# Folding the inverse of modes 0 to 31 into x ahead of the channel product, and adding modes 32 to 63 on row halves in the last stage

## The chip, the cores and the metric

The kernel runs on one core of one Trainium2 chip. The metric is the device time of one execution in microseconds (us). A profile is one execution recorded by the hardware profiler; its span is about 2 us shorter than the device time of the same execution.

## The reference, cut to what matters

A linear attention gives x, a Fourier stage mixes the channels of the first 64 frequencies (modes), and a channel product with a rectifier follows.

```python
num = einsum('bhsd,bhde->bhse', phi(q), einsum('bhsd,bhse->bhde', phi(k), v))
den = einsum('bhsd,bhd->bhs', phi(q), sum(phi(k), axis=2)) + 1e-6
x = (num / den)                       # as [8 batches, 576 rows, 512 channels]
X = rfft(x, axis=1)                   # 64 modes are kept
Y[:, m] = X[:, m] @ (w_r[m] + 1j * w_i[m])      # 64 modes, 512 x 512 each
y = irfft(Y, n=576, axis=1)
u = x + y
out = u + maximum(u @ w_ch, 0)        # float32
```

The weights w_r and w_i are 64 x 2 x 1 MB in float32, by far the largest input. They are converted to bf16 as they are loaded, so 512 KB lands in on-chip memory for each.

## The kernel before

The first 100 us compute the attention and the forward transform. From then on the weights stream in through a ring of eight buffers, and each mode's product is made when its two weights have landed. In the shadow of that stream, 36 tiles of 128 rows and 512 channels are worked on. One tile computes its rows of x again and then forms its channel product E = x @ w_ch, without y:

```python
def channel_product(t):
    num = ...                                        # attention rows (TensorE)
    nc.vector.tensor_tensor(out=x, in0=num, in1=1/den, op=mult)
    nc.scalar.copy(out=x16, in_=x)                   # to f16
    for c in range(4):                               # four transposes
        nc.tensor.transpose(xT_ps[:, c, :], x16[:, c*128 : c*128+128], id16)
    nc.vector.tensor_copy(out=xT, in_=xT_ps)
    for c in range(4):                               # "eps": four products
        nc.tensor.matmul(e_ps, xT[:, c, :], wch16[:, c, :], ...)
    nc.scalar.copy(out=E[t], in_=e_ps)
```

The transform is linear, so y @ w_ch is the inverse transform of Z = Y @ w_ch. A "row building" (`form_rows`, one for each batch) makes Z by four products and y's rows by four transposes, and keeps both in YZ[b]. The last eight modes come too late for this; their rows are made at the very end in a tile called `last` and copied into the rows of YZ[b] by eight small transfers. The last stage then goes over 18 pairs of tiles:

```python
acc  = E                    # by a product with the identity
acc += inv^T @ Z[b]         # all 64 modes are 128 rows (real and imaginary part)
acc  = relu(acc)            # ScalarE
acc += inv^T @ Y[b]
x    = acc + x              # VectorE
store x                     # 512 KB for a pair
```

Where tiles and row buildings stand among the modes is written in this loop, but a scheduler decides the order in which each engine finally executes them, except for instructions that are marked with `pin`, which keep the order of the program:

```python
for kk in range(10, 64):
    mode(kk)                                   # pinned from mode 60 on
    want = min(36, (kk - 10 + 1) * 36 // 42)   # 36 tiles over modes 10 to 51
    while done < want:
        channel_product(tiles[done]); done += 1
    if kk >= 55:
        ...                                    # two row buildings for a mode
```

While the last four modes wait for their weights, 39 needless products (`keep_warm`, called fillers here; their result is never read) keep TensorE busy.

## Time and profile before

| before | | where it is read |
|---|---|---|
| time | 432.05 us, median of 3 (431.16 to 432.51) | the runs |
| span | 429.8 us | the page |
| share of the chain of waits that is DMA | 67% | the page, part 4 |
| a mode's two weight loads | 4.92 us | starts of neighbouring modes' products |
| last stage, from its first product with `last` to the end | 32.2 us (397.62 to 429.8) | the chain of waits |

These are lines of the page of before. In the first four, each place is one of 40 equal slices of the span: the busy share of TensorE and its granted clock in tenths, that of the DMA engines, and what these moved. The fifth line is the chain of waits by engine. The last is the stores of the pairs: how many, how large, and the median time in us from issue to landing.

```profile
PE   0358776887018776856886666778675758999993
PEclk9999666565558765566556678555658655999998
DMA  8999999999999999999999999999999999995697
GB/s 148 207 208 209 209 210 210 211 214 215 222 211 214 215 213 214 214 214 214 213 213 214 214 213 214 213 214 214 213 213 214 214 214 214 214 213 97 239 369 296
...
DMA 67%; PE 17%; issue 7%; DVE 4%; ACT 2%; POOL 1%; DVEq 0%; POOLq 0%; ACTq 0%
...
out_dram<-x_main SPq DMA_DIRECT2D x14, 512.0 KB, 3.1
```

The DMA engines are busy in every slice up to the 36th, which ends at 387 us, so up to there the kernel lasts as long as its weights. TensorE is mostly busy for 50 to 90% of a slice in that time, often at little over half its clock, and this costs nothing.

The chain of waits of before shows how the weights hand over to the last stage (start, duration in us, what):

```profile
340.80 19.27 DMA wi<-in_moe_w_i_dram
...
360.11 0.66 PE P L355 x3
360.77 1.82 PE eps L507 x4
362.59 1.71 PE z L530 x4
...
378.95 0.65 PE P L355 x5
```

The chain meets its last weight load at 360 us. After that TensorE always has work: the last tile (`eps`), eight row buildings (`z`), the last modes (`P`) and the fillers. It is hardly behind the weights; the last mode's product is done at 395.7 us.

In the last stage three limits lie close together. The timeline of before (start, duration, engine, line, operation, operands, count) shows it:

```profile
412.44 0.59 PE L593 MATMUL acc<-E,id 128*128 128x512 f16 x2
412.87 1.03 PE L549 MATMUL acc<-YZ,inv_sb 128*128 128x512 f16 x4
413.73 0.59 PE L593 MATMUL acc<-E,id 128*128 128x512 f16 x2
...
411.35 8.99 DVE L638 TENSOR_TENSOR x_main<-acc,x_main 128x1024 f32<-128x1024 f32 x7
```

A pair takes TensorE 413.73 - 412.44 = 1.29 us, and VectorE 8.99 / 7 = 1.28 us. The stores need 512 KB for a pair, which is 1.28 us at 408 GB/s, about the most that this trace has in a window of 2 us.

### The profile page before, as it was taken

What the parts mean: (1) busy time and instruction counts of PE and PEld (TensorE: products, weight loads), DVE (VectorE), ACT (ScalarE), POOL (GpSimd) and SP (SyncE); (2) the same over time, 40 slices, a digit from 0 to 9 for tenths busy, and PEclk for the clock granted to TensorE, in tenths of its full rate; (3) what the DMA queues carried; (4) which work ended last, traced back from release to release, by engine and by line L of the source; (5) the groups of instructions that cost most, each with busy time, mean ns of one, the idle gap of its engine ahead of it and who ended that gap; (6) DMA issues with size and microseconds to landing.
All of it is one profiled execution on the core that took longest, in us unless ns stands there. A gap on an engine that the chain in (4) does not pass through costs nothing.

```text
span 429.8 us, 6238 instructions
## 1 busy us (share of the span) xinstructions
PE 296.9 (69%) x2551; PEld 154.8 (36%) x2551; DVE 181.9 (42%) x373; ACT 146.6 (34%) x227; POOL 91.5 (21%) x165
## 2 busy tenths in 40 slices
PE   0358776887018776856886666778675758999993
PEld 0346555664003332322232222322222324954441
DVE  1699998955004233233232322332323322211694
ACT  3687666631002222222222322122212222311782
POOL 4232223222102312121112221221211121110200
PEclk9999666565558765566556678555658655999998
DMA  8999999999999999999999999999999999995697
GB/s 148 207 208 209 209 210 210 211 214 215 222 211 214 215 213 214 214 214 214 213 213 214 214 213 214 213 214 214 213 213 214 214 214 214 214 213 97 239 369 296
DMA packets 35803, 92.38 MB, mean 215 GB/s; under 512 B 3136, under 2 KB 16448, under 8 KB 35776
## 3 DMA queue, kind: packets, MB, share of 16 engines
q0 software_dynamic: 32000, 82.00, 98.2%
q1 hardware_dynamic: 3776, 10.00, 6.1%
q8 instruction: 20, 0.33, 0.3%
q14 instruction: 7, 0.06, 0.0%
HBM read 164.07 MB, written 9.44 MB: 404 GB/s over the span
## 4 chain that ended last, share of the span: by engine, by line
DMA 67%; PE 17%; issue 7%; DVE 4%; ACT 2%; POOL 1%; DVEq 0%; POOLq 0%; ACTq 0%
DMA wi<-in_moe_w_i_dram 33%; DMA wr<-in_moe_w_r_dram 22%; DMA k<-in_k_dram 11%; PE acc L549 4%; PE P L355 3%; PE z L530 2%; PE zl L340 2%; PE acc L593 2%; PE eps L507 2%; PE yp L534 1%; DVE x L272 1%; ACT ke L187 1%; DVE k L194 0%; ACT qT L223 0%; POOL q L169 0%
## 5 line engine op out<-in xcount | busy, mean ns | idle before, releaser
L507 PE MATMUL eps<-wch,xTw 128*128 128x512 f16 x144 | 62.3, 582 | 3.4 <-DVE xTw L504 3.1
L515 ACT CAST E<-eps 128x512 f16<-128x512 f32 (+1 forms) x40 | 21.3, 543 | 122.7 <-PE eps L507 122.7
L115 POOL DMA_DIRECT2D wr<-in_moe_w_r_dram x64 | 34.0, 531 | 135.5 <-PE P L355 109.4
L355 PE MATMUL P<-wi,xt_c 128*32 128x512 bf16 x252 | 42.1, 565 | 27.3 <-DMA wi<-in_moe_w_i_dram 27.3
L355 PE MATMUL P<-wr,xt_c 128*32 128x512 bf16 x252 | 42.6, 582 | 22.9 <-DMA wr<-in_moe_w_r_dram 20.9
L115 POOL DMA_DIRECT2D wi<-in_moe_w_i_dram x65 | 34.5, 531 | 108.5 <-PE P L355 74.1
L355 PEld LDWEIGHTS <-xt_c 128*32 128x32 bf16 x504 | 24.3, 163 | 67.8 <-issue 38.7
L369 DVE CAST ys<-P 128x512 f16<-128x512 f32 x32 | 22.0, 688 | 59.7 <-PE P L355 59.7
L151 PEld LDWEIGHTS <-qT 64*128 64x128 f16 (+1 forms) x640 | 21.5, 126 | 56.8 <-issue 41.8
L371 ACT CAST ys<-P 128x512 f16<-128x512 f32 x31 | 18.1, 585 | 63.2 <-PE P L355 63.0
L373 PE MATMUL yt<-pick_sb,ys 128*128 128x16 f16 x252 | 16.8, 177 | 31.6 <-DMA pick_sb<-row_pick 20.4
L504 DVE COPY xTw<-xTp 128x512 f16<-128x512 f16 x36 | 15.2, 423 | 51.8 <-PE xTp L502 51.8
L373 PEld LDWEIGHTS <-ys 128*128 128x128 f16 x252 | 12.3, 105 | 51.1 <-issue 23.4
L151 PE MATMUL num<-kv,qT 64*128 64x65 f16 (+1 forms) x320 | 14.0, 230 | 22.6 <-ACT kv L247 20.1
L507 PEld LDWEIGHTS <-xTw 128*128 128x128 f16 x144 | 14.7, 124 | 33.7 <-issue 24.2
L492 DVE TENSOR_TENSOR x_main<-nw,rd 128x256 f32<-128x256 f32 x32 | 12.1, 419 | 33.8 <-PE nw L151 33.7
L187 ACT ACTIVATE qe<-q 128x1152 f16<-128x1152 f16 x16 | 17.7, 1155 | 22.9 <-DMA q<-in_q_dram 22.9
L216 PE MATMUL qTp<-id,qe 128*128 128x128 f16 x144 | 16.6, 310 | 12.1 <-DVE qe L200 11.7
L499 ACT CAST x16w<-x_main 128x512 f16<-128x512 f32 x32 | 19.8, 619 | 14.2 <-DVE x_main L492 14.2
L272 DVE TENSOR_TENSOR x<-num,rd 128x512 f16<-128x512 f32 x32 | 22.1, 691 | 1.1
L491 DVE RECIPROCAL rdw<-nw 128x4 f32<-128x4 f32 (+1 forms) x40 | 5.5, 170 | 38.3 <-PE nw L151 38.2
L502 PE MATMUL xTp<-id,x16w 128*128 128x128 f16 x144 | 19.4, 278 | 2.8 <-ACT x16w L499 2.4
(71 smaller groups left out, 413.7 us busy)
## 6 DMA issues: line engine op xcount, KB each, us to landing
wr<-in_moe_w_r_dram POOLq DMA_DIRECT2D x64, 512.0 KB, 18.6
wi<-in_moe_w_i_dram POOLq DMA_DIRECT2D x63, 512.0 KB, 18.6
out_dram<-x_main SPq DMA_DIRECT2D x14, 512.0 KB, 3.1
q<-in_q_dram POOLq DMA_DIRECT2D x8, 576.0 KB, 13.5
k<-in_k_dram POOLq DMA_DIRECT2D x8, 576.0 KB, 14.7
v<-in_v_dram POOLq DMA_DIRECT2D x8, 576.0 KB, 16.9
out_dram<-x_main SPq DMA_DIRECT2D x4, 256.0 KB, 3.4
out_dram<-x_tail SPq DMA_DIRECT2D x2, 512.0 KB, 3.4
```

Source lines behind the costliest of these rows:

```text
L115: tc.keep_in_program_order(nc.gpsimd.dma_start(out=w[:, dcs], in_=rows_of[:, dcs, :]))
L151: mm = nc.tensor.matmul(num[hpo][orow, c0 : c0 + 65], qT[rows, hpp, h2, cols], kv_sb[rows, hpp, h2, :])
L187: pin(nc.scalar.activation(out=ev[:, c], in_=heads(nm, b)[:, c], func=AF.Exp))
L272: nc.vector.tensor_tensor(out=dst.rearrange("p (o c d) -> p o c d", o=2, c=4), in0=nv[:, :, :, 0:64], in1=rden.unsqueeze(3).broadcast_to([ ...
L355: mm = nc.tensor.matmul(P[i][dc * 32 : dc * 32 + 32, :], xt_cols(dc, t, kk), w[:, dc, i * pw : i * pw + pw], start=(t == 1), stop=(t == 0) ...
L369: nc.vector.tensor_copy(out=dst, in_=P[i])
L371: nc.scalar.copy(out=dst, in_=P[i])
L373: mm = nc.tensor.matmul(yt_ps[:, ec, kk % 8, :], st[:, ec * 128 : ec * 128 + 128], pick_sb)
L499: nc.scalar.copy(out=x16, in_=x)
L502: nc.tensor.transpose(xT_ps[:, c, :], x16[:, c * 128 : c * 128 + 128], id16)
L507: nc.tensor.matmul(e_ps, xT[:, c, :], wch16[:, c, :], start=(c == 0), stop=(c == NDC - 1))
L515: nc.scalar.copy(out=dst, in_=e_ps[:, cols])
```

## The change

The intent is to make the last stage shorter. If the inverse of modes 0 to 31 is already in x when the channel product is made, E contains it, and the last stage has to add only modes 32 to 63. These are 64 rows instead of 128, so the inverse products of a pair's two tiles can sit on different halves of the TensorE array and run at the same time. For that, YZ[b] holds the same 64 rows twice, on partitions 0 to 63 and on 64 to 127. The four whole tiles of batch 0, the first to be finished, have 56 modes folded in. Two constants are built on the chip (one load of 144 KB is saved), and the fillers fall from 39 to 17.

```diff
+    def early_rows(b, nm):                 # y's rows of modes 0..nm-1
+        for ec in range(NDC):
+            nc.tensor.transpose(y_ps[:r, ec, :], yt, id16)
+        nc.vector.tensor_copy(out=ye[:r], in_=...)

-    def channel_product(t: int):
-        num = ...                          # attention rows, now a function of its own
+    def channel_product(t: int, nm: int):
+        for b, jj, orow in parts_of(t):
+            if (b, nm) not in YE:
+                YE[b, nm] = early_rows(b, nm)
+            nc.tensor.matmul(              # "ya"
+                acc[orow, :], inv_sb[: 2 * nm, rows_of(jj, BASE[b % 2])], YE[b, nm][: 2 * nm, :]
+            )
+        nc.vector.tensor_tensor(out=x, in0=acc, in1=x, op=ALU.add)
         ...                                # cast, transposes, copy, products as before

     def form_rows(b: int):
+        for h in range(2):                 # both partition halves: 8 products, 8 transposes
             for ec in range(NDC):
                 nc.tensor.matmul(
-                    z_ps[: 2 * NE, :], lhs[ec], wch16[:, ec, :], ...
+                    z_ps[HALVES[h], :], lhs[ec], wch16[:, ec, :], ...

     # last stage
-                mm(acc[r, :], inv_sb[:, sel], YZ[b][:, half, :])
+                    g = HALVES[i]          # i: which tile of the pair
+                    mm(i, orow, inv2_sb[g, sel_rows], YZ[b][g, half, :])

     # the loop over the modes
+    forms = {56: (1,), 57: (2,), 58: (3, 4), 59: (5, 6), 60: (7, 0)}
     for kk in range(n_early, NM):
         mode(kk)
-        want = ...; channel_product(tiles[done])
+        if kk < NF:                        # modes 10 to 31: attention rows only
+            for t in a_tiles[spread(...)]: attention_rows(t)
+        elif kk < NE:                      # modes 32 to 55: 32 tiles
+            for t in b_tiles[spread(...)]: channel_product(t, NF)
+        elif kk < NE + 4:                  # modes 56 to 59: batch 0's four tiles
+            channel_product(c_tiles[kk - NE], NE)
+        for b in forms.get(kk, ()): form_rows(b)
```

The late rows now need 16 small transfers, two for each batch, instead of eight.

More of the change, by code (lines that the diff above doesn't have):

```diff
@@ L18, with _dft_consts @@
 NP = 64
-def _dft_consts(S: int, NM: int, NL: int, NB: int):
+def _dft_consts(S: int, NM: int):
     m = np.arange(NM)
@@ L37, in _dft_consts @@
             pick[quad * 32 + c, c] = 1.0
-    inv0 = np.zeros((NL, 2, NB, S), dtype=np.float64)
-    inv0[:, :, 0, :] = inv[NM - NL :]
-    return (
-        fwd.astype(np.float16), inv.reshape(2 * NM, S).astype(np.float16),
-        inv0.reshape(2 * NL * NB, S).astype(np.float16), pick,
-    )
+    return fwd.astype(np.float16), inv.reshape(2 * NM, S).astype(np.float16), pick
 @with_exitstack
@@ L70 @@
     NE = NM - NL
-    fwd_np, inv_np, inv0_np, pick_np = _dft_consts(S, NM, NL, B)
+    NF = NM // 2
+    fwd_np, inv_np, pick_np = _dft_consts(S, NM)
     id16_dr = nc.inline_tensor(np.eye(128, dtype=np.float16), name="ident16")
@@ L75 @@
     inv_dr = nc.inline_tensor(inv_np, name="dft_inv")
-    inv0_dr = nc.inline_tensor(inv0_np, name="dft_inv_first")
     pick_dr = nc.inline_tensor(pick_np, name="row_pick")
@@ L362, in mode_product @@
             if t == 1 and kk >= NM - 4:
-                keep_warm(6)
+                keep_warm(FILL[kk][0])
         if NM - 4 <= kk < NM - 1:
-            keep_warm(3)
+            keep_warm(FILL[kk][1])
         for i in range(n_part):
@@ L378, in mode_product @@
         if NM - 4 <= kk < NM - 1:
-            keep_warm(3)
+            keep_warm(FILL[kk][2])
+    FILL = {60: (0, 0, 0), 61: (3, 2, 1), 62: (5, 2, 2), 63: (2, 0, 0)}
     def last_mode(ps):
@@ L400, in last_mode @@
         product(1, wr, range(NDC))
-        keep_warm(3)
+        keep_warm(FILL[kk][0])
         product(0, wi, range(3))
@@ L421 @@
     inv_sb = ystage.tile([2 * NM, S], F16, name="inv_sb")
+    inv2_sb = ystage.tile([128, S], F16, name="inv2_sb")
     inv0_sb = ystage.tile([128, S], F16, name="inv0_sb")
+    sel = ystage.tile([128, 2, 128], F16, name="row_sel")
     nc.sync.dma_start(out=inv_sb, in_=inv_dr.ap())
-    nc.sync.dma_start(out=inv0_sb, in_=inv0_dr.ap())
+    nc.vector.memset(sel, 0.0)
+    for h in range(2):
+        nc.vector.tensor_copy(out=sel[:, 0, h * 64 : h * 64 + 64], in_=id16[:, 2 * NF : 128])
+    nc.vector.tensor_copy(out=sel[:, 1, 0:128:B], in_=id16[:, 2 * NE : 128])
     YT = ystage.tile([128, NDC, NM, 2 * B], F16, name="YT")
+    nc.vector.memset(YT[:, :, NE:NM, :], 0.0)
     yt_ps = None
@@ L450 @@
     YZ = [sW.tile([128, 2, D], F16, tag="YZ", bufs=B, name=f"YZ{b}") for b in range(B)]
+    YE: dict[int, object] = {}
     E0: dict[int, object] = {}
@@ L473, with parts_of, attention_rows @@
     last_ps = []
-    def channel_product(t: int):
-        num = [bank(f"nw{t}_{o}") for o in range(2)]
-        tail = t >= B * NJJ
-        if tail:
-            i = t - B * NJJ
-            parts = [(2 * i + h, NJJ, slice(h * 64, h * 64 + 64)) for h in range(2)]
-        else:
-            parts = [(t // NJJ, t % NJJ, slice(0, 128))]
+    for i, dst in enumerate((inv2_sb, inv0_sb)):
+        for cols in (slice(0, 512), slice(512, S)):
+            r_ps = bank(f"rows{i}_{cols.start}")[:, 0 : cols.stop - cols.start]
+            nc.tensor.matmul(r_ps, sel[:, i, :], inv_sb[:, cols])
+            nc.scalar.copy(out=dst[:, cols], in_=r_ps)
+    def parts_of(t: int):
+        if t < B * NJJ:
+            b, jj = divmod(t, NJJ)
+            return [(b, jj, slice(0, 128))]
+        p = t - B * NJJ
+        return [(2 * p + h, NJJ, HALVES[h]) for h in range(2)]
+    def attention_rows(t: int):
+        num = [bank(f"nw{t}_{o}") for o in range(2)]
         x = x_of(t)
-        for b, jj, orow in parts:
+        for b, jj, orow in parts_of(t):
             nv = num_matmuls(num, orow, q_view(qT_all[b]), kv_all[b], rows_of(jj, BASE[b % 2]))
@@ L494, in channel_product, with early_rows @@
                     in0=nv[o][:, :, 0:64],
-                    in1=rden.unsqueeze(2).broadcast_to([64 if tail else 128, 4, Dh]),
+                    in1=rden.unsqueeze(2).broadcast_to([orow.stop - orow.start, 4, Dh]),
                     op=ALU.mult,
                 )
+    def early_rows(b: int, nm: int):
+        r = 2 * nm
+        y_ps = bank(f"ye{b}_{nm}", [128, NDC, 128], F16)
+        for ec in range(NDC):
+            yt = YT[:, ec, 0:nm, :].rearrange("p m (t b) -> p (m t) b", b=B)[:, :, b]
+            nc.tensor.transpose(y_ps[:r, ec, :], yt, id16)
+        ye = sW.tile([128, D], F16, tag="YE", bufs=2, name=f"YE{b}_{nm}")
+        nc.vector.tensor_copy(out=ye[:r], in_=y_ps[:r].rearrange("p c r -> p (c r)"))
+        return ye
+    def channel_product(t: int, nm: int):
+        x = x_of(t)
+        acc = bank(f"ya{t}")
+        for b, jj, orow in parts_of(t):
+            if (b, nm) not in YE:
[4 more added lines that the diff above has]
+        nc.vector.tensor_tensor(out=x, in0=acc, in1=x, op=ALU.add)
         x16 = sW.tile([128, D], F16, tag="x16w", bufs=2, name=f"x16w{t}")
@@ L509, in channel_product @@
             )
-        need = {t // NJJ} if not tail else {2 * i, 2 * i + 1}
-        for b in sorted(need):
+        for b, _, _ in parts_of(t):
             if b not in E0:
@@ L515, in channel_product @@
             nc.scalar.copy(out=dst, in_=e_ps[:, cols])
-    tiles = []
+    a_tiles, b_tiles = [], []
     for i in range(B // 2):
-        tiles += [2 * i * NJJ + jj for jj in range(NJJ)] + [B * NJJ + i]
-        tiles += [(2 * i + 1) * NJJ + jj for jj in range(NJJ)]
+        mains = [[(2 * i + h) * NJJ + jj for jj in range(NJJ)] for h in range(2)]
+        a_tiles += mains[0] + [B * NJJ + i] + mains[1]
+        b_tiles += (mains[0] if i > 0 else []) + [B * NJJ + i] + mains[1]
+    c_tiles = list(range(NJJ))
     def form_rows(b: int):
@@ L526, in form_rows @@
         lhs = [
-            YT[:, ec, 0:NE, :].rearrange("p m (t b) -> p (m t) b", b=B)[:, :, b] for ec in range(NDC)
+            YT[:, ec, NF:NM, :].rearrange("p m (t b) -> p (m t) b", b=B)[:, :, b] for ec in range(NDC)
         ]
-        for ec in range(NDC):
-            nc.tensor.matmul(
-                z_ps[: 2 * NE, :], lhs[ec], wch16[:, ec, :], start=(ec == 0), stop=(ec == NDC - 1)
-            )
-        for ec in range(NDC):
-            nc.tensor.transpose(y_ps[: 2 * NE, ec, :], lhs[ec], id16)
@@ L535, in form_rows @@
-        nc.scalar.copy(out=YZ[b][: 2 * NE, 1, :], in_=z_ps[: 2 * NE, :])
-        nc.vector.tensor_copy(
-            out=YZ[b][: 2 * NE, 0, :], in_=y_ps[: 2 * NE].rearrange("p c r -> p (c r)")
-        )
-    last = sW.tile([128, 2, D], F16, tag="last", bufs=1, name="last")
-    EARLY, LATE, BOTH = 1, 2, 3
-    def add_inverse(n: int, i: int, t: int, half: int, what: int = BOTH):
-        acc = accs[n][:, i]
-        mm = lambda o, l, r: on_bank(
-            n, {i}, nc.tensor.matmul(o, l, r, start=False, stop=True, skip_group_check=True)
-        )
-        if t < B * NJJ:
-            b, jj = divmod(t, NJJ)
-            parts = [(b, slice(0, 128), rows_of(jj, BASE[b % 2]))]
-        else:
-            p = t - B * NJJ
-            parts = [
-                (2 * p + h, slice(h * 64, h * 64 + 64), rows_of(NJJ, BASE[h])) for h in range(2)
-            ]
-        for b, r, sel in parts:
-            if what == BOTH:
-                mm(acc[r, :], inv_sb[:, sel], YZ[b][:, half, :])
-                continue
-            if what & EARLY:
-                mm(acc[r, :], inv_sb[: 2 * NE, sel], YZ[b][: 2 * NE, half, :])
-            if what & LATE:
-                mm(acc[r, :], inv0_sb[:, sel], last[:, half, :])
@@ new lines, in form_rows @@
+        for h in range(2):
+            for ec in range(NDC):
+                nc.tensor.matmul(
+                    z_ps[HALVES[h], :], lhs[ec], wch16[:, ec, :], start=(ec == 0), stop=(ec == NDC - 1)
+                )
+        for ec in range(NDC):
+            for h in range(2):
+                nc.tensor.transpose(y_ps[HALVES[h], ec, :], lhs[ec], id16)
+        nc.scalar.copy(out=YZ[b][:, 1, :], in_=z_ps)
+        nc.vector.tensor_copy(out=YZ[b][:, 0, :], in_=y_ps.rearrange("p c r -> p (c r)"))
@@ new lines, with add_inverse, mm @@
+    last = sW.tile([128, 2, D], F16, tag="last", bufs=1, name="last")
+    def add_inverse(n: int, half: int):
+        def mm(i, orow, l, r):
+            on_bank(
+                n, {i},
+                nc.tensor.matmul(
+                    accs[n][orow, i], l, r, start=False, stop=True, skip_group_check=True
+                ),
+            )
+        for i, t in enumerate(pairs[n]):
+            for b, jj, orow in parts_of(t):
+                sel_rows = rows_of(jj, BASE[b % 2])
+                if n < N_PRE:
+                    mm(i, orow, inv0_sb[:, sel_rows], last[:, half, :])
+                else:
+                    g = HALVES[i]
+                    mm(i, orow, inv2_sb[g, sel_rows], YZ[b][g, half, :])
@@ L599, in rectified @@
     def rectified(n: int):
-        for i, t in enumerate(pairs[n]):
-            add_inverse(n, i, t, 1, LATE if n < N_PRE else BOTH)
+        add_inverse(n, 1)
         for i in range(2):
@@ L624, in finish @@
         t0 = pairs[n][0]
+        add_inverse(n, 0)
         for i, t in enumerate(pairs[n]):
-            if n < N_PRE:
-                add_inverse(n, i, t, 0, EARLY)
-                add_inverse(n, i, t, 0, LATE)
-            else:
-                add_inverse(n, i, t, 0)
             if single:
@@ L639, in finish, with spread @@
         store(t0, 2)
-    done = 0
-    rows_done = 0
-    n_spread = NE - 4 - n_early
+    def spread(n_items: int, step: int, steps: int):
+        return slice(n_items * step // steps, n_items * (step + 1) // steps)
+    forms = {56: (1,), 57: (2,), 58: (3, 4), 59: (5, 6), 60: (7, 0)}
     for kk in range(n_early, NM):
         mode(kk)
-        want = min(len(tiles), (kk - n_early + 1) * len(tiles) // n_spread)
-        while done < want:
-            channel_product(tiles[done])
-            done += 1
-        if kk >= NE - 1:
-            while rows_done < min(B, 2 * (kk - NE + 2)):
-                form_rows(rows_done)
-                rows_done += 1
-        if kk == NM - 5:
+        if kk < NF:
+            for t in a_tiles[spread(len(a_tiles), kk - n_early, NF - n_early)]:
+                attention_rows(t)
+        elif kk < NE:
+            for t in b_tiles[spread(len(b_tiles), kk - NF, NE - NF)]:
+                channel_product(t, NF)
+        elif kk < NE + 4:
+            channel_product(c_tiles[kk - NE], NE)
+        for b in forms.get(kk, ()):
+            form_rows(b)
+        if kk == NE + 4:
             psB.release()
@@ L660 @@
                 channels(n)
-                for i, t in enumerate(pairs[n]):
-                    add_inverse(n, i, t, 1, EARLY)
             last_ps.append(psW.tile([128, D], F32, tag="zl", bufs=1, name="zl0"))
@@ L687 @@
         eng = nc.sync if b in (1, 2) else nc.gpsimd
-        eng.dma_start(out=YZ[b][2 * NE : 128, :, :], in_=last[b::B, :, :])
+        for h in range(2):
+            eng.dma_start(out=YZ[b][64 * h + 48 : 64 * h + 64, :, :], in_=last[b::B, :, :])
     psW.release()
```

## The prediction

> **What bounds the kernel now.** The chain of waits is 67% DMA, nearly all weight loads; the DMA row of the slices is full up to about 391 us. A mode (two 512 KB loads) passes every 4.92 us: the wi load of mode 56 is met at 360.1 us, mode 59's would be at about 375, mode 63's lands at about 394. From 360 us TensorE is busy (timeline: row building, mode products, 39 fillers of 0.22 us), hardly late against the weights. The last stage runs from 397.6 us to the end, 32 us: per pair of tiles 6 matmuls x 0.215 = 1.29 us on TensorE, 1.28 us on VectorE (seven adds in 8.99 us), 1.07 us on ScalarE, and stores at up to 408 GB/s, 1.28 us for 512 KB. Three limits coincide.
>
> **What the change gains.** The row halves can at best run two inverse matmuls at once: 4 slots, 0.86 us per pair. VectorE and the stores still need 1.28, so the stage gains only its start (no EARLY matmuls, about 1 us) and the gaps at the tail tiles (about 1 us): 32 becomes about 30.5 us. The dropped constant saves 144 KB at 214 GB/s, 0.7 us.
>
> **What it costs.** All 36 channel products now wait for mode 31, and each gains an addition (matmul, then a VectorE add of about 0.69 us). The built program's order on TensorE decides: there the modes stand ahead of their tiles, one tile per mode, so 13 tiles (9 ordinary, 4 of batch 0) and six of the eight row buildings stand between the products of modes 59 and 60. The Trainium skill (TensorE: Matmul & The Clock Gate, Step-by-step) says that only weight loads are pulled ahead and matmuls stay in program order; the before trace agrees, TensorE waiting for weights ahead of later work.
>
> These tiles stand one behind the other: addition, VectorE add, ScalarE cast, transposes, VectorE copy, four products. From the trace at full clock: 0.38 + 0.69 + 0.62 + 0.40 + 0.43 + 0.86 + about 0.27 of handovers = 3.65 us; at half clock (products 1.7, transposes 0.61, addition 0.65) 5.0. Before, it hid behind the weights. TensorE would be about half busy, and the page's clock section says idle lowers the clock; the trace has 0.54 to 0.75 between 160 and 360 us. I take 4.9 us for nine tiles, 4.5 for four.
>
> A row building has eight products instead of four: about 2.8 us at full clock (before 1.68), 3.2 here.
>
> Sum (estimate): mode 59 at 377; nine tiles 44; two batch changes 2.8; four tiles 18; six buildings 19: mode 60 at about 461. Its product, two buildings and E copies 7.4, modes 61 to 63 7.7, last rows 1.7: 478. Last stage 30.5: span 508, at a better clock 485.
>
> **Prediction: 504 us, range 482 to 526.** Faster by over 2%: 0.02, within 2%: 0.02, slower: 0.96.
>
> **What would show it.** Slices: DMA full to 391 us, then nearly empty for 70 to 90. The chain of waits: from about 375 us no weight load, but 13 tiles at 3.7 to 5 us each. Mode 60's product over 60 us after its weights. The last stage: TensorE below 80% busy, about 30 us long.
>
> **What would make it wrong.** If the chip's order is not the built order, tiles fit between modes: about 428. If the clock stays full in the serial part, about 485. If it halves in the last stage, 4 us more.

## The result, and the profile after

The time after is 504.42 us, the median of four runs (502.62 to 505.61), against 431.69 us for before in the same rounds (431.16 to 432.51). The ratio is 1.168, with a 95% interval of 1.164 to 1.172. Ratios in this text are the mean time of one kernel's fast runs over that of the other's fast runs of the same rounds, so they are not quite the ratio of the medians that are quoted. The result of the changed kernel is correct.

These are the page's lines of after that answer to those of before:

```profile
PE   0378777830966565333779687887785655879992
PEclk9986676755785555555565857575755555579997
DMA  9999999999999999999999999999999000000297
GB/s 159 207 208 211 209 208 213 213 218 212 213 213 214 213 213 214 213 214 213 213 214 214 213 214 214 213 214 213 214 214 207 14 1 0 0 1 0 97 396 301
...
DMA 58%; PE 22%; DVE 9%; issue 4%; ACT 3%; POOL 2%; DVEq 0%; ACTq 0%; POOLq 0%
...
out_dram<-x_main SPq DMA_DIRECT2D x14, 512.0 KB, 4.6
```

The slices are 12.6 us long here. The weights came as fast as before and had all landed by about 393 us: the last of them were issued at 377 us and took 16 us. Then six slices follow in which the DMA engines move next to nothing, with TensorE at least half busy, and at half its clock in the first four. The kernel is doing something else than waiting for data. The chain of waits of after shows what:

```profile
381.65 0.56 PE ya L528
...
382.24 0.70 DVE x_main L531
...
383.02 0.63 ACT x16w L533
...
383.69 0.62 PE xTp L536 x4
...
384.33 0.44 DVE xTw L538
...
384.82 1.89 PE eps L541 x4
386.70 0.56 PE ya L528
...
430.11 1.92 PE z L566 x8
...
456.37 0.62 PE P L350 x6
```

One tile is a chain through three engines, 386.70 - 381.65 = 5.05 us long, and the next tile starts when it is done. There are 13 such tiles between the products of mode 59 (its second half starts at 375.93 us) and of mode 60 (456.30 us), and six row buildings. Nothing in them waits for a weight. Mode 60's product does not wait for a weight either: it stands behind them in TensorE's order and started over 60 us after the last weight load had landed. The other three modes, the last rows and the whole last stage follow from it.

The last stage, for which the change was made, takes 503.8 - 471.81 = 32.0 us against 32.2. These are lines of its timeline after:

```profile
481.23 0.75 PE L582 MATMUL acc<-YZ,inv_sb 64*64 64x512 f16 x6 [0.54 <-DMA YZ<-last]
...
484.32 0.60 PE L621 MATMUL acc<-E,id 128*128 128x512 f16 x2
484.86 0.75 PE L582 MATMUL acc<-YZ,inv_sb 64*128 64x512 f16 x4
...
484.47 9.65 DVE L661 TENSOR_TENSOR x_main<-acc,x_main 128x1024 f32<-128x1024 f32 x8
```

The four inverse products of a pair take 0.75 us instead of 1.03, and the adds follow each other every 9.65 / 8 = 1.21 us instead of 1.28. The last add ends 24.8 us after the stage began, 2.2 us sooner than before (26.95). But from there to the end it takes 7.2 us instead of 5.2. The stores lag behind the adds: at the median a store lands 4.6 us after its issue instead of 3.1, and the last one is issued 1.2 us after the last add has ended (at 497.8 us), where before it was issued at once. The windows view, which gives the busy times, clock and traffic of a stretch of time, has the DMA engines at 408 GB/s from 480 to 494 us; before, in the corresponding 404 to 420 us, it has 368.

### The profile page after: what moved, and what is told of

The parts are those of the page before. It is cut to its first block, busy times and chain, and to the rows that moved or that the text cites. A ratio compares the mean times of both kernels' runs of the same rounds, so it can differ in the third digit from the quotient of the medians.

```text
span 503.8 us, 6558 instructions
## 1 busy us (share of the span) xinstructions
PE 328.2 (65%) x2665; PEld 161.1 (32%) x2665; DVE 209.0 (41%) x423; ACT 148.8 (30%) x231; POOL 94.3 (19%) x171
## 4 chain that ended last, share of the span: by engine, by line
DMA 58%; PE 22%; DVE 9%; issue 4%; ACT 3%; POOL 2%; DVEq 0%; ACTq 0%; POOLq 0%
DMA wi<-in_moe_w_i_dram 26%; DMA wr<-in_moe_w_r_dram 22%; PE eps L541 6%; PE P L350 4%; DMA pick_sb<-row_pick 3%; DMA q<-in_q_dram 3%; DMA k<-in_k_dram 3%; PE z L566 3%; PE xTp L536 2%; DVE x_main L531 2%; PE ya L528 2%; ACT x16w L533 2%; DVE x L267 2%; PE acc L582 1%; DVE xTw L538 1%
## 5 line engine op out<-in xcount | busy, mean ns | idle before, releaser
L350 PE MATMUL P<-wi,xt_c 128*32 128x512 bf16 x252 | 44.0, 573 | 35.8 <-DMA wi<-in_moe_w_i_dram 35.7
L350 PE MATMUL P<-wr,xt_c 128*32 128x512 bf16 x252 | 45.9, 593 | 20.7 <-DMA wr<-in_moe_w_r_dram 18.6
L350 PEld LDWEIGHTS <-xt_c 128*32 128x32 bf16 x504 | 25.9, 160 | 73.7 <-issue 54.3
L531 DVE TENSOR_TENSOR x_main<-ya,x_main 128x512 f32<-128x512 f32 x32 | 22.1, 691 | 60.2 <-PE ya L528 60.0
L146 PEld LDWEIGHTS <-qT 64*128 64x128 f16 (+1 forms) x640 | 23.1, 124 | 39.4 <-issue 19.8
L536 PEld LDWEIGHTS <-x16w 128*128 128x128 f16 x144 | 11.1, 120 | 42.4 <-ACT x16w L533 40.6
L528 PE MATMUL ya<-YE,inv_sb 64*128 64x512 f16 (+2 forms) x40 | 22.9, 572 | 1.6 <-DVE YE L518 1.5
```

What stands on the lines that cost most here:

```text
L146: mm = nc.tensor.matmul(num[hpo][orow, c0 : c0 + 65], qT[rows, hpp, h2, cols], kv_sb[rows, hpp, h2, :])
L350: mm = nc.tensor.matmul(P[i][dc * 32 : dc * 32 + 32, :], xt_cols(dc, t, kk), w[:, dc, i * pw : i * pw + pw], start=(t == 1), stop=(t == 0) ...
L528: nc.tensor.matmul(acc[orow, :], inv_sb[: 2 * nm, rows_of(jj, BASE[b % 2])], YE[b, nm][: 2 * nm, :])
L531: nc.vector.tensor_tensor(out=x, in0=acc, in1=x, op=ALU.add)
L536: nc.tensor.transpose(xT_ps[:, c, :], x16[:, c * 128 : c * 128 + 128], id16)
```

## The experiments

Eleven kernels were run. The theory was the prediction's: what costs the time is not the amount of added work but where it stands. The rivals were that the added work itself costs the time, that starting the channel products at mode 32 costs it, and that the throttled clock does.

To see where work stands, the instructions for TensorE were counted in the order in which they were built. Before mode 59's product there stand 36 tiles and eight row buildings in the kernel before, and 22 tiles and no row building in the one after (a 23rd tile's products stand between its two halves, in the trace too).

### Products from mode 32 on, but without the fold

```diff
 (against the changed kernel)
-                    if kk >= NM - 4:
+                    if kk >= NM - 4 or kk == NF - 1:          # mode 31 pinned
-        ... the additions "ya" and the VectorE add, in channel_product
-            nc.tensor.transpose(xT_ps[:, c, :], ...)
+            pin(nc.tensor.transpose(xT_ps[:, c, :], ...))     # behind mode 31
```

> The changed kernel without the fold (no addition to x before the channel product), products still held back until mode 31; wrong result on purpose. The built order leaves 2 tiles and 4 row buildings between modes 59 and 60, where the changed kernel has 13 and 6. My theory (a serial chain of 5 us per tile, piled up behind mode 59 in TensorE's order): mode 60 at about 391 us, total about 441 us. Rival (starting the products at mode 32 is by itself the cost): total stays above 480 us.

It took 432.72 us (ratio to before 1.0017, interval 1.0001 to 1.0034). The result is wrong by design, since modes 0 to 31 are missing (relative error 0.020). In the built order 34 tiles stand before mode 59's product and all 36 before mode 60's, and mode 60's product starts at 382.9 us. The timeline has it:

```profile
382.90 0.48 PE L350 MATMUL P<-wr,xt_c 128*32 128x512 bf16 x4
```

So a late start of the 36 channel products costs nothing by itself: without the addition they fit between the modes, in this run with the transposes pinned. The expected 441 us was too high, because mode 60's product was expected at 391 us. The two tiles and four row buildings between modes 59 and 60 ran at full clock, the buildings in 1.4 to 1.5 us each from the start of one to the start of what follows.

### The same order, with TensorE kept busy

```diff
 (against the changed kernel, for the 13 tiles behind mode 59)
             nc.tensor.matmul(acc[orow, :], inv_sb[...], YE[b, nm][...])   # pinned
+        if warm:
+            keep_warm(7)
             ...
             nc.tensor.transpose(xT_ps[:, c, :], ...)                      # pinned
+        if warm:
+            keep_warm(2)
```

> The changed kernel with 7 filler matmuls after the addition and 2 after the transposes of the 13 piled-up tiles, same order otherwise; result correct. My theory: the chain per tile shortens only by its TensorE parts, from 5.05 to about 3.7 us, and the row buildings from 2.36 to about 1.7: total about 484 us. Rival (the half clock is the whole cause): near 435 to 445 us. A second rival (TensorE has too much to do): no gain, since fillers add work.

It took 486.04 us (1.125, interval 1.123 to 1.127) and is correct. The chain of waits of one tile now reads:

```profile
403.30 0.34 PE ya L531
403.63 1.62 PE warm L335 x7
405.25 0.29 PE xTp L541 x4
...
405.56 0.43 DVE xTw L545
...
406.04 1.04 PE eps L548 x4
407.08 0.34 PE ya L531
```

A tile takes 3.78 us instead of 5.05. The windows view has the clock at 1.00 from 376 to 440 us, where the changed kernel has 0.50 for 400 to 430 us. Its lines give the stretch, its length, the busy time (and instructions) of PE, PEld, DVE, ACT and POOL, the granted clock, the DMA share and GB/s; first the changed kernel, then this run:

```profile
400.00:430.00 30.00, 18.32 (x57) 6.13 (x57) 6.43 (x12) 6.62 (x12) 0.00 (x0) 0.50 0.00 1
```

```profile
376.00:440.00 64.00, 61.91 (x380) 30.77 (x380) 18.46 (x36) 19.80 (x34) 0.56 (x2) 1.00 0.26 51
```

So the throttled clock is about 18 of the 73 us that were lost. The larger part remains at full clock: it is the chain and its place.

### The same additions, one step per mode

Here each tile's work is cut in four steps (y's rows; addition; transposes; products), and one mode's turn does four steps of four different tiles. TensorE's part of them is pinned, so that they stay between the modes. The work is the same to the instruction: 2665 matmuls in both pages.

```diff
+    def advance():
+        if 0 <= n < len(steps):     rows_step(*steps[n])
+        if 0 <= n - 1 < len(steps): add_step(*steps[n - 1])
+        if 0 <= n - 2 < len(steps): turn_step(steps[n - 2][0])
+        if 0 <= n - 3 < len(steps): product_step(steps[n - 3][0])
         ...
-                channel_product(t, NF)
+                advance()
```

> The changed kernel with the same instructions, but the tile's steps written as a software pipeline (rows, addition, transposes and products of four successive tiles per turn). Built order: 32 of 36 tiles before mode 59, 4 tiles and 2 buildings between modes 59 and 60. My theory (order and serial waits): total about 440 us, range 432 to 448, TensorE's work unchanged. Rival (the added TensorE work itself is what costs, about 31 us more busy time): stays above 480 us.

It took 437.16 us (1.012, interval 1.0095 to 1.0145) and is correct. So 67 of the 73 us go without any of the added work being taken out, and the rival that the additions cost the time by themselves falls. Cutting and pinning come together in this run; no run pins the tiles without cutting them, so their shares are not known. In the built order 32 tiles and four row buildings stand before mode 59's product. The chain of waits around mode 60:

```profile
378.00 0.26 PE yt L368 x4
378.25 0.24 PE ya L534
378.50 0.23 PE xTp L546 x4
378.72 0.86 PE eps L555 x4
...
386.29 0.63 PE P L350 x7
```

The steps of three tiles stand directly behind one another, since none waits for another, and `eps` takes 0.86 us at full clock instead of 1.89. Mode 60's product starts at 386.3 us, 4.0 us later than in before (382.25), which is most of the 5.3 us that are left.

### The fold early, its work spread as before

This kernel folds only modes 0 to 7, so that the additions can start at mode 10, and spreads the tiles over modes 10 to 51 as the kernel before does. It leaves modes 8 to 31 out (8 to 55 in batch 0's four whole tiles), so it is wrong by design; the comparison still passed it, as their share is below its tolerance.

```diff
-        ... attention_rows / channel_product(t, NF) / channel_product(t, NE) by stretches
+        want = min(len(a_tiles), (kk - n_early + 1) * len(a_tiles) // (NE - 4 - n_early))
+        while done < want:
+            attention_rows(a_tiles[done])
+            channel_product(a_tiles[done], 8)
+            done += 1
```

> The changed kernel's chain (fold, then channel product), but begun at mode 10 at the pace of the kernel before, folding modes 0 to 7 only; wrong result on purpose. The built order leaves 7 tiles and 6 row buildings between modes 59 and 60. My theory (the lengthened serial chain makes the scheduler fall behind, wherever it starts): mode 60 at about 424 us, total about 470 us, range 462 to 478. Rival (the late start at mode 32 is the cost, not the chain): about 432 us.

It took 472.4 us (1.094, interval 1.092 to 1.096; two runs). The tiles stand as early in the program as before's, and still seven of them and six row buildings come between modes 59 and 60, whose product starts at 422.6 us. This is the line of its chain of waits:

```profile
422.62 0.62 PE P L350 x5
```

So the dependence on mode 31 is not needed for a loss: 41 of the 73 us are there without it. The longer chain of a tile is enough for tiles to fall behind the modes in the built order; the next run has its tiles in the same places without the addition, with earlier row buildings and more fillers, and takes 429.56 us. Whether the late start adds the rest of the loss was not separated. Why the scheduler puts a mode ahead of a tile that was written before it was not tested; that it does so is read from the order.

The chain of waits here gave another number: at full clock a row building takes 0.93 us for its eight products and 0.41 us for its eight transposes, 1.34 us in all. Before, with half as many of each, it took 1.68.

### The new last stage alone

This is the changed kernel without the fold, with its tiles and row buildings placed as in before and before's fillers. It is wrong by design as the first experiment is (0.020).

```diff
-    FILL = {60: (0, 0, 0), 61: (3, 2, 1), 62: (5, 2, 2), 63: (2, 0, 0)}
+    FILL = {60: (6, 3, 3), 61: (6, 3, 3), 62: (6, 3, 3), 63: (3, 0, 0)}
-        ... the additions
-    forms = {56: (1,), 57: (2,), 58: (3, 4), 59: (5, 6), 60: (7, 0)}
+    forms = {55: (1, 2), 56: (3, 4), 57: (5, 6), 58: (7, 0)}
```

> The schedule of the kernel before (products from mode 10 on, its fillers, its row building times) with the changed last stage on row halves and no fold; wrong result on purpose. My theory (last stage limited by VectorE adds and stores): within 2 us of before, about 430 us, with TensorE less busy there and stores continuous at about 400 GB/s. Rival (TensorE was the limit there, 2 slots of 0.215 us saved per pair, 18 pairs): about 424 us.

It took 429.56 us (0.9956, interval 0.9939 to 0.9973). The last stage runs from 395.9 to 427.2 us, 31.3 us, so it gained 0.9 us against before; the rest is that it began sooner. (The profiled run is the fastest of its six.) Had TensorE been the limit, the expectation has 424 us. TensorE waited once for a small transfer of late rows, at the place where the change has the same wait of 0.54 us (timeline, then windows of 2 us):

```profile
406.06 0.75 PE L574 MATMUL acc<-YZ,inv_sb 64*64 64x512 f16 x6 [1.30 <-DMA YZ<-last]
```

```profile
404.00:406.00 2.00, 0.75 (x6) 0.41 (x5) 1.51 (x2) 1.07 (x2) 0.00 (x0) 1.00 1.01 390
406.00:408.00 2.00, 1.95 (x15) 0.61 (x15) 1.13 (x1) 1.36 (x3) 0.00 (x0) 1.00 1.02 414
```

While TensorE stood still, the stores went on at 390 GB/s. That suggested that the stores set the pace, and the next run tests it.

### The small transfer sooner

```diff
-    for b in (1, 2, 3, 4, 5, 6, 7, 0):
+    for b in (1, 2, 3, 0, 4, 5, 6, 7):     # batch 0's late rows are copied fourth, not last
```

> halves_only with the late-row copies of batch 0 issued third instead of last; wrong result on purpose. In halves_only TensorE waits 1.30 us for that copy at the first tail pair. My theory (stores at 400 GB/s bound the stage from 404 us on): the wait goes, the total changes by less than 0.5 us. Rival (the adds bound the stage): about 1.3 us less, 428.3 us.

It took 429.61 us (0.9956, interval 0.9942 to 0.997), which is the same time, and the wait of 1.30 us is gone from the trace. But the profiled run lost about as much at the start of the stage: the first four inverse products ran at a lowered clock (0.50 in the window of 397 to 399 us, against 1.00), and the first store was issued at 399.98 us instead of 398.73. The first line is of the run above, the second of this one:

```profile
395.87 1.05 PE L574 MATMUL acc<-last,inv_sb 128*128 128x512 f16 x4 [0.30 <-DVE last L696]
```

```profile
396.05 1.90 PE L574 MATMUL acc<-last,inv_sb 128*128 128x512 f16 x4 [0.29 <-DVE last L696]
```

So the equal times do not settle which engine was the limit. That the stores bound the shortened stage is supported by their rate over 404 to 420 us (before, then the run above), but it is not shown by an experiment:

```profile
404.00:420.00 16.00, 16.00 (x83) 7.52 (x81) 14.68 (x13) 12.71 (x25) 0.00 (x0) 1.00 0.92 368
```

```profile
404.00:420.00 16.00, 14.26 (x82) 3.89 (x80) 14.52 (x13) 12.85 (x24) 0.00 (x0) 1.00 1.02 404
```

VectorE is close behind. In the changed kernel it adds without a pause from 484.47 to 494.12 us and hands over 512 KB every 1.21 us, an estimated 435 GB/s from these two figures, where the stores went at 408; that is how they come to lag.

### A version that is correct and tries to keep the gain

Four kernels combine the fold in steps with a placement in which all 36 tiles and all eight row buildings stand before mode 60. They pin every mode from 32 on and differ in their fillers and in the order of the small transfers.

```diff
 (best_b, against the one with one step per mode)
-                    if kk >= NM - 4:
+                    if kk >= NF:                   # products pinned from mode 32 on
-    forms = {56: (1,), 57: (2,), 58: (3, 4), 59: (5, 6), 60: (7, 0)}
+    forms = {56: (1, 2), 57: (3, 4), 58: (5, 6), 59: (7, 0)}
-        if kk == NE + 4:
+        if kk == NE + 3:
+        ... the steps of the first 32 tiles end three modes sooner, those of batch 0 follow two at a time
 (best_c, against best_b)
-    for b in (1, 2, 3, 4, 5, 6, 7, 0):
+    for b in (1, 2, 3, 0, 4, 5, 6, 7):
 (best_d, against best_b: no fillers)
+    FILL = {60: (0, 0, 0), 61: (0, 0, 0), 62: (0, 0, 0), 63: (0, 0, 0)}
 (best_e, against best_b: eleven fillers, none between a mode's two products)
+    FILL = {60: (0, 3, 0), 61: (0, 3, 0), 62: (0, 3, 0), 63: (2, 0, 0)}
```

> The pipelined kernel with its tiles spread over modes 32 to 53, the pipeline emptied before mode 55, row buildings two per mode from mode 56, and mode products kept in program order with the tiles. Built order: all 36 tiles and 8 row buildings stand before mode 60. Correct. My theory: the weights set the pace to mode 63 again, last stage from about 397 us: total 429 us, range 427 to 432. Rival (the added work of TensorE must cost somewhere): above 434 us.

> best_b with the late-row copies of batch 0 issued third instead of last. Correct. My theory (stores bound the last stage): within 0.5 us of best_b. Rival (adds bound it): 1.3 us less.

> best_b without its 17 filler matmuls in modes 61 to 63. Correct. In best_b mode 60's product stands at 380.6 us by the weights, but mode 63's last product comes at 396.2 us, about 3 us after its weights can be there (halves_only met them at 393.1), with TensorE busy on fillers in between. My theory: that product at about 393.5 us, total about 430 us, 2 to 3 us less than best_b. Rival (without fillers the clock falls and the tail slows): no gain, 433 us or more.

> best_d with 11 fillers put only where TensorE waits for a cast (three after the product of modes 60, 61 and 62, two before the last). Correct. In best_d the last product met its weights at 393.0 us but the eight products of the last rows took 1.89 us instead of 1.05, half clock. Theory (no filler delays a weight, the clock stays full): those products 1.05 us again, last product still at about 393.1 us, total about 429.5 us, 1.5 to 2 us less than best_d. Rival (the tail is bounded by the stores alone, which start no earlier): unchanged, 431.3 us.

All four are correct.

| kernel | median us | ratio to before | 95% interval |
|---|---|---|---|
| best_b, 17 fillers | 432.89 | 1.0028 | 1.0012 to 1.0044 |
| best_c, transfers reordered | 433.4 | 1.0033 | 1.002 to 1.0047 |
| best_d, no fillers | 431.31 | 0.9986 | 0.9969 to 1.0004 |
| best_e, 11 fillers | 430.07 | 0.9971 | 0.995 to 0.9992 |

The first missed its 429 us. best_c was within 0.5 us of it, as expected, but best_b's wait for the small transfer was only 0.21 us, so this says little about the stores. Mode 60's product was at 380.6 us, in time, but the fillers then delayed the following modes, and the last mode's product came at 396.2 us. Without fillers (best_d) that product met its weights at 393.0 us, but TensorE was idle before it, and the eight products that follow it took 1.89 us instead of 1.05, with a mean clock of 0.64 from 390 to 396 us. best_e was made to keep the clock with fewer fillers; it did (1.05 us), though its last product was at 395.5 us. By its median it is the best correct kernel, 0.3% faster than before, with an interval that ends just below 1. What its fillers are worth is not settled: its six runs lie in two groups, near 429.7 and near 431.9 us, and the profiled one is of the slower group, while best_d's profiled run was the fastest of its six (429.93 us).

### Before with fewer fillers

The gain of the kernels above could come from the fillers alone, so before was run with 14 of its 39.

```diff
-                keep_warm(6)       # after w_r's product
+                keep_warm(2)
-            keep_warm(3)           # after the mode's product, and after its last step
+            keep_warm(1)
-        keep_warm(3)               # in the last mode
+        keep_warm(2)
```

> The kernel before with 14 fillers in modes 60 to 63 instead of 39. Correct. In the kernel before, mode 63's last product starts at 395.0 us without a wait for its weights; in halves_only they were met at 393.1. Theory: 1 to 1.5 us less than before, about 430.5 us. Rival (the fillers only use time that TensorE would spend waiting): unchanged, 431.8 us.

It took 432.68 us (1.0025, interval 1.0012 to 1.0038) and missed its 430.5. The last product met its weights, with a wait of 0.34 us, but the next line of the timeline shows the price. The first line is of this run, the second, in a fence of its own, of before:

```profile
394.43 1.89 PE L674 MATMUL zl<-wch,YT 128*128 128x256 f16 x8 [0.32 <-DVE YT L404]
```

```profile
395.97 1.05 PE L674 MATMUL zl<-wch,YT 128*128 128x256 f16 x8 [0.32 <-DVE YT L404]
```

The same eight products took 1.89 us instead of 1.05, as in best_d, and the mean clock from 390 to 396 us was 0.55. They began 1.5 us sooner, and 0.8 us of that was lost in them. This profiled run was the fastest of the five (431.34 us), so where the slower ones lost more is not seen. What holds is that fewer fillers in before gain nothing. The two kernels with the new last stage and before's fillers, at 0.4%, do not owe their gain to fewer fillers anyway; for best_e, whose fillers stand in other places, it stays open.

## Why the prediction was right

The predicted 504 us stands against 504.42 measured, the median of the four device times. The prediction's own sum gave a span of 508 us with the tiles mostly at half clock, and 485 at a better one; the sum can be compared term by term with the profiled span of 503.8 us, which is of the slowest of the four runs.

| term of the sum | predicted, us | measured, us | difference |
|---|---|---|---|
| mode 59 done | at 377 | at 376.5 | -0.5 |
| nine tiles and the first change of batch (a tail tile, with new rows and a second addition) | 44 + 1.4 | 47.3 (376.54 to 423.80) | +1.9 |
| second change of batch | 1.4 | 1.2 | -0.2 |
| four tiles of batch 0 | 18 | 18.7 | +0.7 |
| six row buildings | 19 | 12.6 | -6.4 |
| mode 60, two buildings, copies of E | 7.4 | 6.0 (456.30 to 462.29) | -1.4 |
| modes 61 to 63 | 7.7 | 7.7 | 0 |
| last rows | 1.7 | 1.8 | +0.1 |
| last stage | 30.5 | 32.0 | +1.5 |

(The six buildings are 2.36, 2.36, 4.30 for two and 3.58 for two, added from the chain of waits; the four tiles are what remains of 425.02 to 456.30.)

- **The order decides: right, and shown.** Thirteen tiles and six buildings stand between modes 59 and 60, as read from the built order. The page "TensorE: Matmul & The Clock Gate" of the Trainium skill, section "Step-by-step: what each phase is for", says "The MATMULs themselves stay in program order", and this trace agrees: mode 60's product started over 60 us after its weights, behind work that did not need them. The run with the same work in another order took 437 us.
- **A tile is a chain of 5.0 us at half clock, taken as 4.9: right, and slightly small as taken.** It measured 5.05 us. Its waits between engines are as predicted, one `VectorE` add of 0.70 us and one cast of 0.63 us among them.
- **The clock would mostly be halved: right.** The windows view has 0.50 for 400 to 430 us, and 0.55 for 377 to 456. (The prediction gives 0.54 to 0.75 for before between 160 and 360 us; the last 20 us of that have 0.51.) The run with fillers puts the clock's share at 18 of the 73 us.
- **"A row building has eight products instead of four: about 2.8 us at full clock", 3.2 in this place: this is the step that was mis-sized most.** It measured 1.34 us at full clock and 2.36 at half clock. I counted the products of the two partition halves one after the other, but they write different column halves of the array and ran side by side: eight took 1.92 us at half clock, and four whole ones 1.89. The page "TensorEngine Tiling (Array Packing)", section "Key Properties", says that different tiles can execute in parallel, and the trace agrees. I had used just this for the last stage and not for the buildings.
- **"at best two inverse matmuls at once: 4 slots, 0.86 us per pair": not reached.** Where TensorE was not held back, at 478.99 us, a pair took 1.10 us, and in the steady part 1.2. The same section says that changing the tiling mode drains TensorE. That fits: two copies of E, which use the whole array, took 0.54 us between row-half products against 0.43 in before. No run separated this cost.
- **The last stage of 30.5 us: mis-sized.** It measured 32.0. The prediction had named the stores among the limits, at 408 GB/s, and yet took what the adds gain, about 2 us at the start and at the tail tiles, as a gain of the stage. The adds ended 2.2 us sooner and the stores took 2.0 us more after them. TensorE was 83% busy (20.0 of 24 us from 474 to 498 us) while the pairs ran; the predicted "below 80%" holds only with the wait for the last stores (22.18 of 32 us), and so it does in before (24.95 of 32.2 us).
- **What the profile was to show:** the DMA engines full to 391 us and then nearly empty for 70 to 90 us was right (80 us); no weight load in the chain of waits after 375 us was right too.

The hit owes something to errors that cancelled: the buildings were 6.4 us too long in the sum, the tiles and the last stage 4 us too short, and the number given, a device time, was about 6 us below the sum, whose span of 508 us is about 510 us of device time.

## What to carry to other kernels

A step that waits for nothing but itself is harmless in the shadow of a long transfer and costs its full length when the order of an in-order engine puts it ahead of work that the transfer has already released; so when a change lengthens a chain, read the order in which each engine will execute it, and not the sum of the work. If the added work must stay, cut it into steps of different tiles between the pieces of the paced work: here that brought back 67 of 73 us with the same 2665 matmuls. And before speeding up one engine in a stage where several limits coincide, look at what the others have left: here stores at 368 GB/s had about 10% to give, and a stage whose four inverse products fell from 1.03 to 0.75 us became 0.2 us shorter.

## What the Trainium skill lacked or had wrong

- "TensorE: Matmul & The Clock Gate", "Why this matters for your kernels", advises against idle gaps of more than about 3 us between bursts of matmuls. Here the longest idle within a tile was 1.49 us, TensorE was busy for 3.09 of 5.10 us (61%), and the granted clock was 0.50 throughout 400 to 430 us. In best_b, from 320 to 340 us, TensorE was busy for 15.53 of 20 us (78%) and had a clock of 1.00. So the absence of long gaps is not enough for the full clock. The row above it asks for 4 us of unbroken work, and the longest unbroken stretch of a tile here is 2.4 us (`eps` and the next `ya`), so the page is not contradicted there. Nor does the busy share decide by itself: the run with TensorE kept busy has 17.80 of 20 us (89%) at a clock of 0.50 from 340 to 360 us, before its fillers begin.
- "DMA: Bandwidth & Descriptors", section "Where 436 GB/s comes from", says that the HBM side, about 358 GB/s, binds transfers between HBM and on-chip memory (the same passage counts 425 GB/s as measured for a load). With one core running, the stores here went at 408 GB/s over 14 us, and at 418 over 2 us. "HBM Reference", "Specifications (TRN2)", which gives about 425 for a core that streams alone, fits the runs.
- "TensorEngine Tiling (Array Packing)", "Key Properties", names the drain between tiling modes without a duration. Two whole-array products took 0.54 us between row-half products against 0.43 us among whole-array ones, which is a hint of it and not a measurement of the drain alone.
- No page says that a scheduler may place work that waits for no weights behind the modes that do, nor how to see it. Here 13 of 36 tiles and six row buildings came to stand behind mode 59, and the kernel took 73 us longer.
